# Gated linear attention and a squared-ReLU layer on one core: casting DMA for w_in, transposes moved off TensorE, PSUM banks given out by the scheduler

## The chip, the cores and the metric

The kernel runs on one core of a Trainium2 chip. The metric is the device time of one execution in microseconds (us). Engines are named as in the profile: PE (TensorE matmul), PEld (its weight loads), DVE (VectorE), ACT (ScalarE), POOL (GpSimd), SP (SyncE, which here only issues DMAs).

## The reference

Per batch (4) and head (8), over 768 steps with 48 channels, a state of 48 x 48 decays by alpha and takes up k v; y is q times the state. The heads side by side are x, 3072 tokens of 384, and a layer follows:

```python
for t in range(S):
    state = alpha[:, :, t, :, None] * state + np.einsum('bhd,bhe->bhde', k[:, :, t], v[:, :, t])
    y[:, :, t] = np.einsum('bhd,bhde->bhe', q[:, :, t], state)
...
h = x @ w_in                 # 384 -> 2048
r = np.maximum(h, 0.0)
g = s * (r * r) + b
return (g @ w_out).astype(np.float32)   # 2048 -> 384
```

Inputs and output are float32.

## The kernel before, in words

Tokens go in 24 blocks of 128 (six per batch; block 0, 6, 12 and 18 are the first of a batch). Each block n has one attention part of these steps, four pairs of heads side by side:

- st_ln (ACT, L275): logarithm of alpha. st_cum (PE, L281, L286): its running sum over the block by a triangular matrix, and the sum of all 128 rows, one column for each head pair. st_exp_b and st_exp_i (ACT, L295 to L299): decays, their inverses, and the block's whole decay.
- st_qb, st_kb (DVE, L308, L313): q and k times decay and inverse. st_vcast (POOL, L302): v to bf16, with zeros between the heads of a pair.
- st_T (PE, L324): eight transposes of q and k into PSUM; st_Tcopy (DVE, L344) brings them to SBUF.
- st_KV (PE, L335): k by v, eight matmuls of 64 output rows; st_t1 and st_snew (DVE L354, L356; POOL L364): the new state.
- st_A (PE, L370) and st_mask (DVE, L379): the scores of a block, masked.
- st_y (PE, L414): y already transposed, channels on the partitions, as 12 narrow matmuls in the first block of a batch and 20 in the others, with output tiles of 64 or 32 rows. st_yevac (ACT, L432): y to the bf16 tile xd of its group.

The layer goes by groups of two or four blocks (GROUPS). mm1 (PE, L454) makes a unit of 1536 columns (three k-steps) in one of two PSUM banks h_ps; relu (ACT, L463) and square (DVE, L471, one instruction for each slice of 128 hidden channels) follow. mm2 (PE, L478) sums a block's output in quads of four matmuls; oevac (DVE, L489) scales it by s and adds the bias (b times the column sums of w_out, L262); ostore (SP, L501) stores it. There are 96 units and 96 quads.

Inputs come by SP in 192 KB DMAs (L175), four a block, in packets of 192 bytes, into five buffers each. w_in and w_out come in pieces of 768 KB (L220, L234) through four float32 staging tiles; POOL casts both (L228, L240). In PSUM, cum and the transposes share one bank, KV and y another, st_A has two, h_ps two, o_ps two.

The order on every engine is made at build time by the class Schedule: each step is an op with an engine, a duration, a priority and the resources that it reads and writes. A list scheduler takes the ready op of lowest priority at the earliest time; want(n) gives block n's due time and LEAD how far ahead of its mm1 it is due. Each engine then works its list in order. LOADS is the order of the first loads.

Of the kernel before, what the change touches and what calls it, by code (L numbers as in the profile page):

```python
# [12 lines left out]

VW = 144

GROUPS = [2, 2, 2, 2, 4, 4, 4, 4]
LEAD = {1: 17.0, 2: 20.0, 4: 18.0}

RING = 12

NST = 4

LOADS = ["b0", "b1", "i0", "i1", "b2", "i2", "b3", "i3", "o0", "o1", "o2", "b4", "o3", "b5", "b6"]

class Schedule:
# [12 lines left out]
    def done(self, res, t):  # L40
        self.preset[res] = t

    def op(self, eng, dur, prio, fn, *args, r=(), w=(), lat=0.1):
        me = len(self.ops)
        deps = set()
        start = 0.0
        for x in r:
            if x in self.writer:
                deps.add(self.writer[x])
            start = max(start, self.preset.get(x, 0.0))  # L50
        for x in w:
            if x in self.writer:
                deps.add(self.writer[x])
            deps.update(self.readers.get(x, ()))
        for x in r:
            self.readers.setdefault(x, []).append(me)
        for x in w:
            self.writer[x] = me
            self.readers[x] = []
            self.preset.pop(x, None)  # L60
        self.ops.append((eng, dur, prio, fn, args, deps, lat, start))

    def run(self):
# [10 lines left out]
        for i, o in enumerate(self.ops):  # L74
            free.setdefault(o[0], 0.0)
            ready.setdefault(o[0], [])
            if not left[i]:
                ready[o[0]].append((o[7], i))
        todo = n
        while todo:  # L80
            best = None
            for e, items in ready.items():
                if not items:
                    continue
                t = max(free[e], min(x[0] for x in items))
                _, i = min((self.ops[i][2], i) for a, i in items if a <= t + 1e-9)
# [4 lines left out]
            eng, dur, _, _, _, _, lat, _ = self.ops[i]  # L91
            begin[i] = t
            free[e] = t + dur
            end[i] = t + dur
            todo -= 1
            for u in users[i]:
                left[u] -= 1
                if not left[u]:
                    a = self.ops[u][7]
# [15 lines left out]
def kernel(  # L115
# [23 lines left out]
    NIN = 5  # L139
# [25 lines left out]

# [5 lines left out]
    b_col = sb.tile([128, 1], FP32, name="b_col")  # L171

# [7 lines left out]
    load(0, alpha, a_in)  # L180
    load(0, q, q_in)
    load(0, k, k_in)
    load(0, v, v_in)
    nc.scalar.preload_act_table_set("natural_log_exp_and_others")

    la_sb = many("la", 2, [128, H, 64], BF16, zero=nc.vector)
    U_bf = sb.tile([128, 128], BF16, name="U_bf")
    make_upper_triangular(nc, U_bf, 1.0, diag=True)
    ident_bf = sb.tile([128, 128], BF16, name="ident_bf")
    make_identity(nc, ident_bf)  # L190
    ones_col_bf = sb.tile([128, 1], BF16, name="ones_col_bf")
    nc.vector.memset(ones_col_bf, 1.0)
    vp_sb = many("vp", 3, [128, NP, VW], BF16, zero=nc.gpsimd)
    mask = sb.tile([128, 128], BF16, name="mask")
    make_upper_triangular(nc, mask, 1.0, diag=True)
    b_sb = many("b_s", 2, [128, H, D], FP32)
    binv_sb = many("binv", 2, [128, H, D], FP32)
    qb_sb = many("qb", 2, [128, H, 64], BF16, zero=nc.vector)
    kb_sb = many("kb", 2, [128, H, 64], BF16, zero=nc.vector)
    qkT_sb = many("qkT", 2, [128, 2, NP, 128], BF16)  # L200
    am_sb = many("am", 2, [128, 2, NP, 128], BF16)
    blast_sb = many("blast", 2, [128, NP], BF16)
    t1_sb = many("t1", 2, [128, NP, 96], BF16)
    s_sb = many("s_st", 2, [128, NP, 96], BF16)
    xd_sb = many("xd", 3, [128, 3, 512], BF16)
    r_sb = many("r", 2, [128, 512], BF16)
    gt_sb = [sb.tile([128, RING * C], BF16, name=f"gt{j}") for j in range(NJ)]
    out_sb = many("o_sb", 3, [128, d_model], FP32)

    w_in_bf = sb.tile([128, 3, d_ff], BF16, name="w_in_bf")  # L210
    w_out_bf = sb.tile([128, NJ, d_model], BF16, name="w_out_bf")
    QW = 4 * d_model
    wst = many("wst", NST, [128, QW], FP32)
    colsum = sb.tile([128, 2 * d_model], FP32, name="colsum")
    colpart = sb.tile([128, 2 * d_model], FP32, name="colpart")
    bones = sb.tile([128, 128], FP32, name="bones")
    bias_w = sb.tile([128, d_model], FP32, name="bias_w")

    def load_w_in(i, st):
        nc.sync.dma_start(  # L220
            out=wst[st].rearrange("a (k f) -> a k f", k=3),
            in_=moe_w_in[:, QW // 3 * i : QW // 3 * (i + 1)].rearrange(
                "(k r) f -> r k f", r=128
            ),
        )

    def cast_w_in(i, st):
        nc.gpsimd.tensor_copy(  # L228
            out=w_in_bf[:, :, QW // 3 * i : QW // 3 * (i + 1)],
            in_=wst[st].rearrange("a (k f) -> a k f", k=3),  # L230
        )

    def load_w_out(i, st):
        nc.sync.dma_start(  # L234
            out=wst[st].rearrange("a (j m) -> a j m", j=4),
# [403 lines left out]
```

## Time and profile before

| | us |
|---|---|
| median of 3 runs | 218.08 |
| lowest, highest | 216.7, 219.16 |
| span of the profiled execution | 215.9 |
| PE busy, share of the span | 190.6, 88% |
| DVE busy | 149.3, 69% |
| ACT busy | 100.8, 47% |
| POOL busy | 47.5, 22% |

The span goes from the first to the last instruction of one profiled execution. The page gives no other time of that execution than its span. Busy time of PE is not PE at its peak: matmuls are pipelined, and a matmul at the lower of the two clock levels is busy for longer.

### The profile page before, as it was taken

The page shows a single profiled execution, that of the slowest core. Times are in us where ns is not written, and L with a number is a line of the kernel's source. Part 1 is how long each engine was busy: PE and PEld are TensorE (multiplying, and loading weights), DVE is VectorE, ACT ScalarE, POOL GpSimd, SP SyncE. Part 2 cuts the span into 40 slices and gives each one's busy share as a digit, 9 for nine tenths or more (in the row PEclk, how much of TensorE's full clock was granted, in tenths as well). Part 3 has the DMA queues.
Part 4 walks back from the last instruction along what each step waited for, and adds up shares of the span by engine and source line. Part 5 has one row for each costly group of instructions (what it writes and reads, how often), then busy time and mean ns, then how long its engine had stood idle before and what let it go on. Part 6 is the DMA issues. An engine that isn't in the chain of part 4 may idle for free.

```text
span 215.9 us, 4933 instructions
## 1 busy us (share of the span) xinstructions
PE 190.6 (88%) x1916; PEld 112.4 (52%) x1916; DVE 149.3 (69%) x283; ACT 100.8 (47%) x217; POOL 47.5 (22%) x65
## 2 busy tenths in 40 slices
PE   0167694959999999999999999999999999999993
PEld 0045462535767677756455555545555555555551
DVE  3187269999978787886898868799686963444321
ACT  2313242245655654633787637776365434444200
POOL 8144446635021212111112211002220100000000
PEclk9999998788999999999999999999999999999999
DMA  6999899999499999999977775230110111111122
GB/s 128 189 328 228 189 355 288 241 179 178 98 205 210 211 199 211 196 208 194 218 151 146 148 170 117 44 78 2 36 39 0 39 36 39 37 38 38 39 73 73
DMA packets 107096, 30.21 MB, mean 140 GB/s; under 512 B 100416, under 2 KB 105536, under 8 KB 107072
## 3 DMA queue, kind: packets, MB, share of 16 engines
q1 hardware_dynamic: 107008, 29.89, 59.6%
q8 instruction: 15, 0.25, 0.5%
q14 instruction: 9, 0.07, 0.1%
q0 software_dynamic: 64, 0.00, 0.0%
HBM read 25.17 MB, written 4.72 MB: 138 GB/s over the span
## 4 chain that ended last, share of the span: by engine, by line
PE 51%; DVE 0%; issue 0%
PE o_ps_69 L478 10%; PE h_ps_66 L454 10%; PE o_ps_68 L478 10%; PE h_ps_67 L454 10%; PE py_ps L414 3%; PE ct_ps L324 2%; PE a_ps L370 2%; PE py_ps L335 2%; PE ct_ps L281 1%; PE ct_ps L286 0%; DVE o_sb_169 L489 0%
## 5 line engine op out<-in xcount | busy, mean ns | idle before, releaser
L454 PEld LDWEIGHTS <-w_in_bf 128*128 128x128 bf16 x384 | 36.0, 102 | 23.9 <-issue 3.1
L463 ACT ACTIVATE r_149<-h_ps_66 128x512 bf16<-128x512 f32 x48 | 28.7, 598 | 36.3 <-PE h_ps_66 L454 33.3
L463 ACT ACTIVATE r_150<-h_ps_67 128x512 bf16<-128x512 f32 x48 | 28.8, 599 | 29.1 <-PE h_ps_67 L454 13.2
L454 PE MATMUL h_ps_66<-xd_147,w_in_bf 128*128 128x512 bf16 (+1 forms) x72 | 16.3, 344 | 1.4 <-ACT r_149 L463 1.4
L454 PE MATMUL h_ps_67<-xd_147,w_in_bf 128*128 128x512 bf16 (+1 forms) x72 | 16.7, 352 | 0.0
L379 DVE TENSOR_TENSOR am_139<-a_ps,mask 128x1024 bf16<-128x1024 f32 x12 | 14.7, 1222 | 2.6 <-PE a_ps L370 2.4
L379 DVE TENSOR_TENSOR am_138<-a_ps,mask 128x1024 bf16<-128x1024 f32 x12 | 14.6, 1220 | 1.8 <-PE a_ps L370 1.5
L454 PE MATMUL h_ps_67<-xd_146,w_in_bf 128*128 128x256 bf16 (+1 forms) x72 | 14.4, 333 | 0.7 <-ACT r_150 L463 0.7
L454 PE MATMUL h_ps_66<-xd_146,w_in_bf 128*128 128x256 bf16 (+1 forms) x72 | 15.0, 344 | 0.0
L364 POOL TENSOR_TENSOR s_st_144<-t_142,blast_140 128x384 bf16<-128x384 bf16 x8 | 7.7, 960 | 23.5 <-DVE t_142 L356 16.3
L344 DVE COPY qkT_136<-ct_ps 128x1024 bf16<-128x1024 bf16 x12 | 8.3, 688 | 6.2 <-PE ct_ps L324 5.7
L281 PE MATMUL ct_ps<-la_97,U_bf 128*128 128x384 bf16 x12 | 4.3, 360 | 9.1 <-ACT la_97 L275 9.1
L364 POOL TENSOR_TENSOR s_st_145<-t_143,blast_141 128x384 bf16<-128x384 bf16 x8 | 7.8, 974 | 15.4 <-DVE t_143 L356 13.3
L344 DVE COPY qkT_137<-ct_ps 128x1024 bf16<-128x1024 bf16 x12 | 8.3, 688 | 4.2 <-PE ct_ps L324 4.1
L454 PE MATMUL h_ps_66<-xd_148,w_in_bf 128*128 128x256 bf16 (+1 forms) x48 | 9.8, 327 | 0.0
L454 PE MATMUL h_ps_67<-xd_148,w_in_bf 128*128 128x256 bf16 (+1 forms) x48 | 9.8, 326 | 0.0
L295 ACT ACTIVATE b_s_124<-ct_ps 128x384 f32<-128x384 f32 x12 | 5.9, 491 | 7.9 <-PE ct_ps L286 7.6
L295 ACT ACTIVATE b_s_125<-ct_ps 128x384 f32<-128x384 f32 x12 | 5.9, 490 | 6.1 <-PE ct_ps L286 5.8
L286 PEld LDWEIGHTS <-la_97 128*128 128x128 bf16 x48 | 3.1, 100 | 8.8 <-issue 8.0
L324 PE MATMUL ct_ps<-ident_bf,qb_128 128*128 128x128 bf16 x48 | 5.2, 236 | 2.3 <-DVE qb_128 L308 2.3
L432 ACT ACTIVATE xd_147<-py_ps 128x384 bf16<-128x384 f32 x10 | 4.9, 493 | 4.7 <-PE py_ps L414 4.5
L308 DVE TENSOR_TENSOR qb_128<-q_in_75,b_s_124 128x384 bf16<-128x384 f32 x3 | 1.7, 552 | 7.7 <-ACT b_s_124 L295 7.7
(209 smaller groups left out, 466.9 us busy)
## 6 DMA issues: line engine op xcount, KB each, us to landing
out_dram<-o_sb_167 SPq DMA_DIRECT2D x8, 192.0 KB, 2.3
out_dram<-o_sb_168 SPq DMA_DIRECT2D x8, 192.0 KB, 2.1
out_dram<-o_sb_169 SPq DMA_DIRECT2D x8, 192.0 KB, 1.9
a_in_70<-in_alpha_dram SPq DMA_DIRECT2D x5, 192.0 KB, 4.0
q_in_75<-in_q_dram SPq DMA_DIRECT2D x5, 192.0 KB, 3.8
k_in_80<-in_k_dram SPq DMA_DIRECT2D x5, 192.0 KB, 3.7
v_in_85<-in_v_dram SPq DMA_DIRECT2D x5, 192.0 KB, 4.1
a_in_71<-in_alpha_dram SPq DMA_DIRECT2D x5, 192.0 KB, 3.9
```

Of the source, the lines that this page charges most:

```text
L281: nc.tensor.matmul(out=cum_ps, lhsT=U_bf, rhs=la[:, :, 0:D], start=True, stop=True)
L295: nc.scalar.activation(out=b_sb[n % 2], in_=cum_ps, func=AF.Exp)
L324: nc.tensor.transpose(out=t_ps[:, x, p, :], in_=f[:, 128 * p : 128 * p + 128], identity=ident_bf,)
L335: nc.tensor.matmul(out=p_ps[64 * e : 64 * e + 64, p, :], lhsT=kb[:, 128 * p + 64 * e : 128 * p + 64 * e + 64], rhs=vp[:, p, 48 * e : 48 * ...
L344: nc.vector.tensor_copy(out=qkT_sb[n % 2].rearrange("a x p t -> a (x p t)"), in_=t_ps.rearrange("a x p t -> a (x p t)"),)
L364: nc.gpsimd.tensor_tensor(out=s_sb[n % 2], in0=t1_sb[n % 2], in1=bl, op=ALU.mult)
L379: nc.vector.tensor_tensor(out=am_sb[n % 2].rearrange("a e p t -> a (e p) t"), in0=a_ps.rearrange("a e p t -> a (e p) t"), in1=mask.unsquee ...
L414: nc.tensor.matmul(out=y_ps[32 * (x % 4) : 32 * (x % 4) + 32 * m, x // 4, :], lhsT=(st[:, p, c0 : c0 + 32 * m] if e is None else vp[:, p, ...
L432: nc.scalar.activation(out=xd_sb[g % 3][:, :, t * C : (t + 1) * C], in_=y_ps, func=AF.Copy)
L454: nc.tensor.matmul(out=hp[:, i * n : (i + 1) * n], lhsT=w_in_bf[:, kk, 128 * j : 128 * (j + 1)], rhs=xd_sb[g % 3][:, kk, 0:n], start=(kk = ...
L463: nc.scalar.activation(out=r_sb[w % 2], in_=h_ps[w % 2], func=AF.Relu)
L478: nc.tensor.matmul(out=op[:, 0:d_model], lhsT=gt_sb[j][:, c0 : c0 + C], rhs=w_out_bf[:, j, :], start=(j == 0), stop=(j == NJ - 1),)
```

## The change

- Groups are now 1, 1, 2, 2, 2, 4, 4, 4, 4 blocks, LEAD is one number, and there are nine input buffers of each kind (NIN). The first loads are now ops of the schedule.
- w_in comes by four DMAs on POOL's queue that cast to bf16 on the way (load_w_in); no staging, no cast on POOL. w_out keeps its staging, with its own tile for each piece, and ACT casts it in two halves (cast_w_out).
- st_KV is four matmuls of full width that also make the cross terms between the two heads of a pair; st_sfirst and st_snew, in two halves of 64 partitions, take only the diagonal blocks into the state. It is left out in the last block of a batch. v is cast densely.
- st_y puts tokens on the partitions: four matmuls of 96 columns on the state and eight of 48 columns on the scores. st_yevac copies it to yn. For blocks 0 to 9 PE then transposes y (st_yT, three transposes) and ACT copies it into xd; from block 10 on (N_PE_T) a DMA transpose on SP does it (st_yTdma).
- From block 10 on, q and k are transposed by one DMA on SP (st_Tdma) in place of eight PE transposes and the DVE copy.
- Six PSUM banks are a pool: the scheduler gives one to each use (c, T, P, y, Y, h, o, b) with a limit on how many of each kind may be held. h may hold three.
- square is one instruction for each unit.
- The scheduler models a DMA queue (dma=, BACKLOG).

```diff
-GROUPS = [2, 2, 2, 2, 4, 4, 4, 4]
-LEAD = {1: 17.0, 2: 20.0, 4: 18.0}
+GROUPS = [1, 1, 2, 2, 2, 4, 4, 4, 4]
+LEAD = 24.0
+UNIT = 1.62
 RING = 12
...
-LOADS = ["b0", "b1", "i0", "i1", "b2", "i2", "b3", "i3", "o0", "o1", "o2", "b4", "o3", "b5", "b6"]
+NIN = 9
+N_PE_T = 10
+
+LOADS = ["b0", "i0", "i1", "b1", "i2", "i3", "b2", "o0", "o1", "o2", "o3", "b3"]
...
+    def load_w_in(i):
+        nc.gpsimd.dma_start(
+            out=w_in_bf[:, :, 512 * i : 512 * (i + 1)],
+            in_=moe_w_in[:, 512 * i : 512 * (i + 1)].rearrange("(k r) f -> r k f", r=128),
+        )
...
+    def cast_w_out(i, e):
+        dst = w_out_bf[:, 4 * i + 2 * e : 4 * i + 2 * e + 2]
+        src = wst[i][:, 768 * e : 768 * (e + 1)].rearrange("a (j m) -> a j m", j=2)
+        nc.scalar.activation(out=dst, in_=src, func=AF.Copy)
...
+    def st_Tdma(n):
+        nc.sync.dma_start_transpose(
+            out=qkT_sb[n % 3].rearrange("a x p t -> a (x p) t"),
+            in_=qk_sb[n % 3].rearrange("a x h d -> a (x h d)"),
+        )
...
+        for p in range(NP):
+            nc.tensor.matmul(
+                out=p_ps[:, p, :],
+                lhsT=kb[:, 128 * p : 128 * p + 128],
+                rhs=vb[:, 96 * p : 96 * p + 96],
+                start=True,
+                stop=True,
+            )
...
+        inter = n % NCH != 0
+        if inter:
+            for p in range(NP):
+                nc.tensor.matmul(
+                    out=y_ps[:, 96 * p : 96 * p + 96],
+                    lhsT=qT[:, p, :],
+                    rhs=st[:, p, :],
+                    start=(p == 0),
+                    stop=False,
+                )
+        for h in range(H):
             nc.tensor.matmul(
...
+                out=y_ps[:, 48 * h : 48 * h + 48],
+                lhsT=am[:, h % 2, h // 2, :],
+                rhs=vb[:, 48 * h : 48 * h + 48],
+                start=(h == 0 and not inter),
+                stop=(h == H - 1),
             )
...
+    def st_yTcopy(n):
+        nc.scalar.activation(out=x_of(n), in_=yt_of(n), func=AF.Copy)
+
+    def st_yTdma(n):
+        nc.sync.dma_start_transpose(out=x_of(n), in_=yn_sb[n % 3])
...
+    sched = Schedule(len(banks), {"c": 2, "T": 1, "P": 2, "y": 2, "Y": 1, "h": 3, "o": 2, "b": 1})
...
+            if n < N_PE_T:
+                op("PE", 0.5, t + 0.3, st_T, n, r=[("qb", i3), ("kb", i3)], w=[("T", n)], lat=0.27,
+                   take=("T", n))
+                op("DVE", 0.61, t + 0.4, st_Tcopy, n, r=[("T", n)], w=[("qkT", i3)], drop=("T", n))
+            else:
+                op("SP", 0.5, -3000, st_Tdma, n, r=[("qb", i3), ("kb", i3)], w=[("qkT", i3)],
+                   lat=1.2, dma=1.1)
```

The order that comes of it, at three places. ACT at the start of the program, before; la is the logarithm of a block's alpha, a_in_70 that of block 0, a_in_71 that of block 1:

```order
L184 ACT_TABLE_LOAD
L275 ACTIVATE la_99<-a_in_71 128x8x48
L275 ACTIVATE la_97<-a_in_70 128x8x48
L295 ACTIVATE b_s_124<-ct_ps 128x384
L298 ACTIVATE binv_126<-ct_ps 128x384
```

ACT at the same place now; yn is y of block 0, xd its transposed copy:

```order
L212 ACT_TABLE_LOAD
L302 ACTIVATE la_109<-a_in_70 128x8x48
L323 ACTIVATE b_s_143<-bank_64 128x384
L326 ACTIVATE binv_145<-bank_64 128x384
L327 ACTIVATE blast_152<-bank_64 128x4
L463 ACTIVATE yn_156<-bank_67 128x384
L302 ACTIVATE la_111<-a_in_71 128x8x48
L479 ACTIVATE xd_159<-bank_68 128x3x128
```

The logarithm of block 1 moved from ahead of block 0's to behind block 0's y.

POOL at the start, before, with what each instruction waits for; b_col and s_col are the scalars b and s on all partitions, bones the bias matrix, vp_113 and vp_115 the cast v of blocks 0 and 1:

```order
L528 DMA b_col<-in_moe_b_dram 128x1
L531 DMA s_col<-in_moe_s_dram 128x1
L255 MEMSET bones 128x128
L256 TENSOR_SCALAR bones<-bones,b_col 128x128 [waits DMASW0_49,Pool_49]
L302 CAST vp_115<-v_in_86 128x4x2x48 [waits DMAHW7_49]
L302 CAST vp_113<-v_in_85 128x4x2x48 [waits DMAHW3_49]
L228 CAST w_in_bf<-wst_172 128x3x512 [waits DMAHW0_49]
L228 CAST w_in_bf<-wst_173 128x3x512 [waits DMAHW1_49]
```

And now:

```order
L255 DMA w_in_bf<-in_moe_w_in_dram 128x3x512 x4
L579 DMA b_col<-in_moe_b_dram 128x1
L582 DMA s_col<-in_moe_s_dram 128x1
L283 MEMSET bones 128x128
L284 TENSOR_SCALAR bones<-bones,b_col 128x128 [waits DMASW4_49,Pool_49]
L330 CAST vb_140<-v_in_97 128x384 [waits DMAHW3_49]
L330 CAST vb_141<-v_in_98 128x384 [waits DMAHW7_49]
```

The four loads of w_in stand ahead of the load of b, and the product that waits for b stands, as before, ahead of the first cast of v.

SP in the middle of the program, before; o_sb is a block's output, the a, q, k and v loads are those of later blocks:

```order
L175 DMA v_in_86<-in_v_dram 128x8x48
L501 DMA out_dram<-o_sb_169 128x384
L175 DMA a_in_72<-in_alpha_dram 128x8x48
L175 DMA q_in_77<-in_q_dram 128x8x48
L175 DMA k_in_82<-in_k_dram 128x8x48
```

And now, where the transposes begin; qkT_148 is that of block 10, v_in_101 the v of block 13:

```order
L249 DMA a_in_74<-in_alpha_dram 128x8x48
L249 DMA q_in_83<-in_q_dram 128x8x48
L366 DMA_TRANSPOSE qkT_148<-qk_122 128x8x128
L249 DMA k_in_92<-in_k_dram 128x8x48
L249 DMA v_in_101<-in_v_dram 128x8x48
L366 DMA_TRANSPOSE qkT_149<-qk_124 128x8x128
L249 DMA a_in_75<-in_alpha_dram 128x8x48
L249 DMA q_in_84<-in_q_dram 128x8x48
L249 DMA k_in_93<-in_k_dram 128x8x48
L366 DMA_TRANSPOSE qkT_147<-qk_120 128x8x128
L550 DMA out_dram<-o_sb_165 128x384
```

The transposes stand among the loads on the one list of SP, each behind the loads of a block some three later.

## Rows read from the trace of the kernel before

**Rows 1.** The page: its span, and the bytes moved in 40 equal slices
```profile
span 215.9 us, 4933 instructions
...
GB/s 128 189 328 228 189 355 288 241 179 178 98 205 210 211 199 211 196 208 194 218 151 146 148 170 117 44 78 2 36 39 0 39 36 39 37 38 38 39 73 73
```

**Rows 2.** Busy time by stretch: stretch, length, PE, PEld, DVE, ACT, POOL, clock, DMA
```profile
0.00:24.80 24.80, 9.33 (x111) 6.25 (x111) 11.43 (x20) 6.84 (x16) 12.63 (x24) 1.00 0.91 218
24.80:50.40 25.60, 19.47 (x173) 12.15 (x170) 22.08 (x34) 8.73 (x19) 11.64 (x9) 0.87 0.95 250
50.40:212.50 162.10, 161.81 (x1638) 93.95 (x1635) 115.22 (x230) 85.26 (x182) 23.21 (x32) 1.00 0.51 112
212.50:215.90 3.40, 0.00 (x0) 0.00 (x0) 0.58 (x1) 0.00 (x0) 0.00 (x0) 1.00 0.16 58
```

**Rows 3.** The chain that ended last, in order of time: start, us, what
```profile
106.83 0.46 PE py_ps L414 x12
107.29 0.75 PE h_ps_66 L454 x3
108.04 0.45 PE ct_ps L324 x8
108.49 0.65 PE h_ps_67 L454 x3
109.14 0.29 PE py_ps L335 x8
109.43 0.75 PE h_ps_66 L454 x3
110.18 0.33 PE a_ps L370 x8
110.51 0.27 PE ct_ps L281
110.78 0.08 PE ct_ps L286 x4
110.86 0.67 PE h_ps_67 L454 x3
...
112.83 0.62 PE py_ps L414 x20
```

**Rows 4.** Groups by line: the bias matmuls (busy us, mean ns, idle before)
```profile
L262 PE MATMUL o_ps_69<-colsum,bones 128*128 128x384 f32 x4 | 1.5, 486 | 0.0
```

**Rows 5.** The instructions of the first 25 us, in order of time
```profile
0.73 0.43 SPq L175 DMA_DIRECT2D a_in_70<-in_alpha_dram  x1
...
8.13 0.52 ACT L275 ACTIVATE la_99<-a_in_71 128x384 bf16<-128x384 f32 x1 [6.13 <-DMA a_in_71<-in_alpha_dram]
...
14.78 0.76 PE L414 MATMUL py_ps<-am_138,vp_113 128*64 128x128 bf16 x12 [0.87 <-DVE am_138 L379]
...
24.85 1.46 PE L454 MATMUL h_ps_66<-xd_146,w_in_bf 128*128 128x256 bf16 x6
```

**Rows 6.** DMA issues of the first 30 us: size, us from issue to landing
```profile
a_in_70<-in_alpha_dram SPq DMA_DIRECT2D x1, 192.0 KB, 2.8
...
b_col<-in_moe_b_dram POOLq DMA_DIRECT2D x1, 0.5 KB, 3.2
```

**Rows 7.** Busy time in the stretch of the block loads
```profile
60.00:110.00 50.00, 49.78 (x592) 32.23 (x590) 40.13 (x85) 27.38 (x61) 8.77 (x13) 1.00 0.98 204
```

**Rows 8.** The instructions of DVE and POOL from 32 us, in order of time
```profile
32.26 2.26 POOL L240 CAST w_out_bf<-wst_172 128x1536 bf16<-128x1536 f32 x1 [0.60 <-DMA wst_172<-in_moe_w_out_dram]
...
33.11 1.55 DVE L471 TENSOR_TENSOR gt_153<-r_150 128x256 bf16<-128x256 bf16 x1
```

**Rows 9.** The page's groups by line: relu
```profile
L463 ACT ACTIVATE r_149<-h_ps_66 128x512 bf16<-128x512 f32 x48 | 28.7, 598 | 36.3 <-PE h_ps_66 L454 33.3
```

**Rows 10.** The page's groups by line: the copy of the transposed q and k
```profile
L344 DVE COPY qkT_136<-ct_ps 128x1024 bf16<-128x1024 bf16 x12 | 8.3, 688 | 6.2 <-PE ct_ps L324 5.7
```

**Rows 11.** The page: the DMA queue of SP (packets, MB, share of 16 engines)
```profile
q1 hardware_dynamic: 107008, 29.89, 59.6%
```

More of the change, by code (lines that the diff above doesn't have):

```diff
@@ L74, in run, with start @@
         for i, o in enumerate(self.ops):
-            free.setdefault(o[0], 0.0)
+            free.setdefault(o[0], 0.7)
             ready.setdefault(o[0], [])
             if not left[i]:
-                ready[o[0]].append((o[7], i))
-        todo = n
+                ready[o[0]].append((0.0, i))
+        idle = {b: 0.0 for b in range(self.banks)}
+        held = {k: 0 for k in self.most}
+        drops = dict(self.drops)
+        until = {}
+        queue = 0.0
+        todo = n
+        def start(a, i):
+            take = self.ops[i][8]
+            if take is None:
+                return a
+            if not idle or held[take[0]] >= self.most[take[0]]:
+                return None
+            return max(a, min(idle.values()))
         while todo:
@@ L203 @@
[L203 to L213, printed above, removed]
@@ new lines, in st_sfirst @@
+    def st_sfirst(n):
+        p_ps = p_of(n)
+        for e in range(2):
+            rows, cols = half(e)
+            nc.vector.tensor_tensor(
+                out=s_sb[n % 2][rows, :, cols],
+                in0=p_ps[rows, :, cols],
+                in1=blast_sb[n % 2][rows].unsqueeze(2).to_broadcast([64, NP, D]),
+                op=ALU.mult,
+            )
+    def st_t1(n):
+        nc.vector.tensor_tensor(
+            out=t1_sb[n % 2], in0=p_of(n), in1=s_sb[(n - 1) % 2], op=ALU.add
+        )
@@ L441 @@
         for u in range(NJ // per):
-            units.append((g, [u * per + i for i in range(per)]))
+            units.append((g, u * per, per))
         for tt in range(m):
@@ new lines @@
+            if not last:
+                op("PE", 0.2, t + 0.35, st_KV, n, r=[("kb", i3), ("vb", i3)], w=[("P", n)], lat=0.27,
+                   take=("P", n))
+            if first:
+                op("DVE", 0.6, t + 0.5, st_sfirst, n, r=[("P", n), ("bl", i2)], w=[("S", i2)],
+                   drop=("P", n))
+            elif not last:
+                op("DVE", 0.48, t + 0.5, st_t1, n, r=[("P", n), ("S", 1 - i2)], w=[("t1", i2)],
+                   drop=("P", n))
+                op("POOL", 1.1, t + 0.1, st_snew, n, r=[("t1", i2), ("bl", i2)], w=[("S", i2)])
@@ L586 @@
             unit_i += 1
[L587 removed]
+            j0 = units[w][1]
+            js = range(j0, j0 + per)
             t = w * UNIT
[L589 to L593 removed]
+            op("PE", 0.66, t, mm1, w,
+               r=[("xd", g % 3, x) for x in range(m)] + [("wib", j0 // 4)],
+               w=[("h", w)], lat=0.27, take=("h", w))
+            op("ACT", 0.5, t + 0.5, relu, w, r=[("h", w)], w=[("r", w % 2)], drop=("h", w))
+            op("DVE", 0.36, t + 1.0, square, w, r=[("r", w % 2)],
                w=[("gt", x, j) for j in js for x in ring])
```

435 lines of the change are left out of this document (209 added, 226 removed), and 5 rows, old and new, of the table Y_PARTS.

## The prediction

> **What bounds the kernel now.** I read the page's slices first, then the stretches, the chain that ended last, the waits of PE, and last the DMA views. [...] From 50.4 us on PE is busy 161.81 of 162.10 us at a granted clock of 1.00, while DVE has 115.22 and ACT 85.26 of it [rows 2]: here only PE's own work counts. [...] After 212.5 us there are 3.4 us of last eviction and store. The DMA engines move 128 to 355 GB/s in the first ten slices, so they hardly pause [rows 1, 2].
>
> The chain tells what a piece of PE work costs when nothing waits: its pieces stand end to end. A unit of mm1 is 0.65 us after full-width work, but 0.75 after st_KV or st_y, whose tiles are 64 or 32 columns wide: a change of tile form costs 0.10. So a block's attention costs: transposes 0.45, st_KV 0.29 + 0.10, st_A 0.33, cum 0.27 + 0.08 (the 0.27 holds the 0.10 behind st_A), st_y 0.62 + 0.10, or 0.46 + 0.10 in the first block of a batch [rows 3]. With 0.02 of rounding that is 2.26, or 2.10 in the four first blocks. PE's whole work before: 24 x 2.26 - 4 x 0.16 = 53.6, 192 units and quads x 0.65 = 124.8, the bias matmuls 1.5 [rows 4]: 179.9 us.
>
> **PE work, removed and added.** The four matmuls of one column behind cum take 0.08 + 0.02, that is 25 ns for a pair of weight load and matmul of full width; a transpose of 128 columns takes 0.45 / 8 = 56 ns [rows 3]. By columns a matmul of 96 costs 42 ns, one of 48 costs 21, for which I take the 25. st_KV has now 4 x 42 = 0.17 and no change of form: -0.22. st_y has 4 x 42 + 8 x 25 = 0.37 for 20 narrow ones: -0.35. Blocks 0 to 9 gain three transposes of y, 3 x 56 = +0.17: together -0.40 a block. Blocks 10 to 23 lose the eight transposes, -0.45: together -1.02. Four last blocks lose st_KV altogether, another 0.17 each. Sum: 10 x 0.40 + 14 x 1.02 + 4 x 0.17 = 19.0 us; 160.9 remain. The bounds of it: if each narrow pair costs the 56 ns of a transpose, st_KV saves 0.17 and st_y 0.05, and the sum is 10.8. Below, with 21 ns, it is 19.8. I take 25 because it is a measured row of the same kind of weights.
>
> [...]
>
> **The start.** Before, the first logarithm on ACT is that of block 1 and waits 6.13 us for its alpha; block 0's y starts at 14.78 and the first mm1, which needs block 1 as well, at 24.85 [rows 5]. Now block 0's logarithm stands first, its alpha lands at 0.73 + 2.8 = 3.5 us [rows 5, 6], and a group of one block needs no second. But this is not what sets the steady part; data are. A load of 192 KB at the 204 GB/s of the stretch full of loads [rows 7] takes 0.96, a block 3.84; a 768 KB piece of weights at the 355 GB/s of the best slice [rows 1] takes 2.2. Bytes begin at about 2.5 (3.5 less one load). Order: b0, w_in, b1, b2, w_out, b3. Block 3 is in at 2.5 + 4 x 3.84 + 8 x 2.2 = 35.5. On PE's list cum of block 6 stands ahead of the first mm1 of blocks 2 and 3, so alpha of block 6 is wanted: 35.5 + 2 x 3.84 + 0.96 = 44.1, then 0.52 of logarithm [rows 5] and 0.7 of cum and st_A ahead of mm1: PE runs on from 45.5.
>
> By then it has done mm1 and mm2 of blocks 0 and 1 (16 x 0.65 = 10.4), the bias 1.5, blocks 0 to 3 (4 x 1.86, less 0.17 in the first) 7.3, parts of 4 to 6 some 2.3: 21.5 us. Left: 139.4.
>
> The casting DMA's price is not in the trace. From below it is the 2.2 of a plain piece; from above, 768 KB at the loads' 204 GB/s, 3.9. I take 2.2, the row of the same piece; the upper end puts the start off by 6.8. POOL: four descriptor jobs stand ahead of b_col, s_col, the bias product and vcast of block 0. The product waits for b_col, 3.2 us to landing before [rows 6] and now behind 3 MB in its queue, so to about 15; behind it wait vcast, KV and y of block 0, and with them, in order, PE. mm1 of block 0 then starts at about 19 and not 12. The cover is the wait for block 6 at 45.5: some 17 us of work are left for 26 us, so I cost it at nothing, at most 3.
>
> POOL's w_out cast stood beside a square of 1.55 us on DVE [rows 8]; both go. The casts on ACT are 8 x 768 columns; at relu's 598 ns for 512 [rows 9] 0.9 each, 7.2 us, hidden in the stretch where ACT is busy 8.73 of 25.6 [rows 2]. One square of 512 columns for two of 256 and no Tcopy in 14 blocks lighten DVE: 115.2 - 14 x 0.69 (its row, [rows 10]) = 105.5 over 139.4, 76%. It still fits, but nearer to PE: I add 2 us of gaps (0 to 4) and 2.5 us of low clock behind the start (19.47 x 0.13, [rows 2]; the same sort of start).
>
> **The DMA transposes.** 256 KB for q and k and 96 KB for y, 14 times, on SP's queue. The trace has none. From below: 352 KB at 355 GB/s, 1.0 us. From above: in pieces of 32 bytes, 11,264 packets at 0.596 x 16 x 215.9 / 107,008 = 19.2 ns each on 16 engines [rows 11], 13.5 us. Between ends so far apart I go by the row of the block loads, 352 KB at 204 GB/s = 1.7, and take 1.6. A block then costs the queues 3.84 + 0.55 (store) + 1.6 = 6.0, PE 5.2 + 1.24 = 6.4: it just fits. Blocks 0 to 9 are in at 2.5 + 17.6 + 38.4 + 1 = 59.5, block 23 at 59.5 + 13 x 6.0 = 138. Its chain (exponentials, transposes, mask, y) is about 13: 151. PE comes to the last group's mm1 45 pieces x 0.65 = 29 us before its end, at about 160. So 9 us of slack. SP takes its list in order: a transpose waits for kb or y of its block, and the loads and stores behind it wait too; nine input buffers instead of five cover that.
>
> [...]
>
> **The sum.** 45.5 + 139.4 + 2.5 + 2 + 3.4 = 192.8 us of span. The page gives only the span of its execution, 215.9; the median of the runs, 218.08, lies 2.2 above it. So 195.
>
> **Rivals.**
> 1. Narrow matmuls cost a full pitch of 56 ns. For it: nothing else in the trace has 48 columns under 128-wide weights. Against: the 25 ns. 10.8 saved and not 19.0: 203.
> 2. The queues set the pace. With T for both transposes of a block the end moves by 13 x (T - 1.6) - 9 once this is positive. T = 3.0 gives 204. For it: 6.0 against 6.4 is no margin, and before the queues are full from 60 to 110 us [rows 7]. Against: the slack.
> 3. Slower: the transposes go in small pieces. Place: SP's queue, blocks 10 to 23; price by the same formula; it passes 218 at T = 4.1 and is 1% slower at 4.2. T = 8 gives 269, 13.5 gives 341. [...] Against: no row; but even the loads, the smallest packets here, move 204 GB/s. [...]
> 4. Better: no gaps, no low clock, the start 2 us earlier: 188.
> That the change doesn't do what it says can only be for its start: the logarithm of block 1 might still hold it, but ACT's list has block 0's first.
>
> **Chances.** Forecast 0.52, rival 1 0.12, rival 2 0.17, rival 3 0.09, rival 4 0.10. The runs before lie 1.1% apart, so 1% is about what a measurement can tell from no change. Faster takes all but rival 3 and the far end of rival 2 (0.03, T about 4): 0.88, within 1% 0.03, slower 0.09. The range reaches from just under rival 4, 187, to rival 2 at T = 3.8, 214; outside stay rival 3, and a few in a hundred at either end.
>
> **What would show it.** PE idle of under 4 us from about 46 us to the end; st_y at about 0.4 and st_KV at 0.2 in the chain; b_col landing near 15 us and vcast of block 0 behind it; transposes landing in 2 to 6 us; PE's waits in the second half for ACT's relu at most. It is wrong if mm1 of a late group waits for a DMA, if the stretch from 140 to 165 us shows idle PE, or if PE starts its steady part past 52 us.

## The result and the profile after

The changed kernel takes 206.67 us (median of 4 runs, 206.11 to 207.96) beside 217.39 (216.22 to 219.16) for the kernel before in the same comparison: a ratio of 0.950 with a 95% interval of 0.944 to 0.956. It is faster, by 10.7 us; the forecast of 195 stood for some 22. Batches of runs are compared below by their ratio to the kernel before; times are medians of all runs, and a ratio leaves out runs over 1.5% above the fastest of their kernel, unless said otherwise.

The page of the changed kernel, its span, PE's line, and the slices of the DMA engines with what they moved; [rows 1] has the same of before:

```profile
span 204.4 us, 4279 instructions
...
PE 167.6 (82%) x1594; PEld 107.4 (53%) x1594; DVE 131.7 (64%) x240; ACT 107.8 (53%) x235; POOL 39.7 (19%) x76
...
DMA  6999999999999999999999799999964221111122
GB/s 131 175 189 195 270 379 209 188 209 227 189 211 188 216 205 191 188 211 178 159 224 184 148 204 206 176 204 209 201 138 109 61 59 40 40 42 38 38 77 77
...
q1 hardware_dynamic: 126016, 31.80, 75.3%
q0 software_dynamic: 1664, 1.57, 4.8%
```

PE's busy time fell from 190.6 to 167.6 us, but its share of the span too, from 88 to 82%: PE has become idle somewhere. The DMA engines stay nearly full until about 148 us (29 of 40 slices). Where PE is idle shows in the stretches, to be held beside [rows 2]; the columns are busy us of each engine with its instructions, granted clock, DMA share and GB/s:

```profile
core 0: us, PE busy (x) PEld busy (x) DVE busy (x) ACT busy (x) POOL busy (x), PEclk, DMA share, GB/s
...
8.40:19.10 10.70, 0.06 (x2) 0.09 (x1) 1.23 (x1) 0.00 (x0) 1.07 (x2) 1.00 1.16 195
19.10:49.65 30.55, 23.89 (x305) 18.88 (x306) 24.59 (x41) 21.08 (x45) 7.46 (x11) 1.00 1.01 246
49.65:81.00 31.35, 31.34 (x407) 25.39 (x408) 30.86 (x55) 24.85 (x62) 9.63 (x17) 1.00 1.00 199
81.00:156.00 75.00, 65.17 (x592) 37.02 (x590) 52.86 (x98) 42.96 (x98) 14.69 (x27) 1.00 0.99 185
156.00:200.97 44.97, 44.93 (x277) 24.59 (x275) 17.85 (x39) 16.16 (x28) 0.00 (x0) 1.00 0.18 56
```

PE works without a pause from 49.65 to 81 us and from 156 us to its end at 200.97. Between them, where the kernel before had 49.78 us of 50 busy as late as 60 to 110 [rows 7], it loses 9.8 of 75.00 us, and the DMA share is 0.99. PE's waits say for what (us in total, times, longest):

```profile
PE bank L376 <- POOL vb L330: 10.7, 1, 10.7
PE a_ps L417 <- DMA qkT<-qk: 9.1, 9, 1.6
```

The second is st_A waiting for a DMA transpose, nine times. The first, the stall in the start, is taken up below. PE's timeline around one of these waits (start, us, line, operation, instructions, idle before and its releaser):

```profile
97.72 0.33 PE L376 MATMUL bank<-vb,qk 128*128 128x96 bf16 x4
97.89 0.81 PE L502 MATMUL bank<-xd,w_in_bf 128*128 128x512 bf16 x3
98.53 0.33 PE L442 MATMUL bank<-s_st,qkT 128*128 128x96 bf16 x4
98.70 0.36 PE L450 MATMUL bank<-vb,am 128*128 128x48 bf16 x8
98.91 0.81 PE L530 MATMUL bank<-w_out_bf,gt 128*128 128x384 bf16 x4
99.56 0.81 PE L502 MATMUL bank<-xd,w_in_bf 128*128 128x512 bf16 x3
101.88 0.40 PE L417 MATMUL a_ps<-qkT 64*128 64x128 bf16 x8 [1.51 <-DMA qkT<-qk]
102.21 0.82 PE L530 MATMUL bank<-w_out_bf,gt 128*128 128x384 bf16 x4
102.87 0.81 PE L502 MATMUL bank<-xd,w_in_bf 128*128 128x512 bf16 x3
```

The differences of the starts are the prices: st_KV 0.17, st_y 0.17 + 0.21 = 0.38, a unit of mm1 0.64; [rows 3] has what they cost before. And at 101.88 the reader sees the loss: st_A of block 14 waits 1.51 us, and behind it stand a quad and a unit that need nothing of this block, but PE's list is in order. Where its transpose was until then is told by DVE's last instruction ahead of it (k times the inverse decay) and by SP's issue of it:

```profile
91.19 0.55 DVE L341 TENSOR_TENSOR qk<-k_in,binv 128x384 bf16<-128x384 f32 x1
97.78 2.05 SPq L366 DMA_TRANSPOSE qkT<-qk  x1
```

Its data are ready at 91.74, SP comes to it 6 us later, at 97.78, and it lands at 101.83. The transposes of q and k of 13 of the 14 blocks stand ready 2 to 8 us before SP issues them; from issue to landing they take 3.1 to 5.6 us.

The chain that ended last goes through the start and through these transposes (start, us, what):

```profile
3.95 2.33 POOL w_in_bf L255 x3
6.29 11.52 DMA b_col<-in_moe_b_dram
17.99 0.61 POOL bones L284
18.60 0.48 POOL vb L330
19.12 0.48 PE bank L376 x4
...
97.78 4.05 DMA qkT<-qk
...
102.10 4.00 DMA qkT<-qk
```

### The profile page after: what moved, and what is told of

Its sections match the earlier page's. It is cut to its first block, busy times and chain, and to the rows that moved or that the text cites. A ratio compares the mean times of both kernels' runs of the same rounds, so it can differ in the third digit from the quotient of the medians.

```text
span 204.4 us, 4279 instructions
## 1 busy us (share of the span) xinstructions
PE 167.6 (82%) x1594; PEld 107.4 (53%) x1594; DVE 131.7 (64%) x240; ACT 107.8 (53%) x235; POOL 39.7 (19%) x76
## 3 DMA queue, kind: packets, MB, share of 16 engines
q1 hardware_dynamic: 126016, 31.80, 75.3%
## 4 chain that ended last, share of the span: by engine, by line
PE 56%; DMA 26%; DVE 7%; issue 4%; POOL 3%; ACT 3%; SPq 0%; POOLq 0%; ACTq 0%; DVEq 0%
PE bank L530 23%; PE bank L502 22%; DMA qkT<-qk 19%; DMA b_col<-in_moe_b_dram 6%; PE a_ps L417 3%; PE bank L353 2%; POOL w_in_bf L255 2%; DMA a_in<-in_alpha_dram 1%; PE bank L450 1%; DVE colpart L272 1%; DVE am L426 1%; PE bank L309 1%; PE bank L376 1%; ACT r L511 1%; DVE gt L523 1%
## 5 line engine op out<-in xcount | busy, mean ns | idle before, releaser
L502 PE MATMUL bank<-xd,w_in_bf 128*128 128x512 bf16 (+2 forms) x432 | 76.5, 315 | 0.7 <-DMA xd<-yn 0.5
L511 ACT ACTIVATE r<-bank 128x512 bf16<-128x512 f32 x96 | 56.6, 604 | 35.7 <-PE bank L502 26.7
L530 PE MATMUL bank<-w_out_bf,gt 128*128 128x384 bf16 x384 | 73.7, 326 | 0.0
L523 DVE TENSOR_TENSOR gt<-r 128x512 bf16<-128x512 bf16 x96 | 41.9, 448 | 23.7 <-ACT r L511 23.3
L530 PEld LDWEIGHTS <-gt 128*128 128x128 bf16 x384 | 35.7, 98 | 25.3 <-issue 0.2
L426 DVE TENSOR_TENSOR am<-a_ps,mask 128x1024 bf16<-128x1024 f32 x24 | 29.3, 1219 | 11.7 <-PE a_ps L417 11.5
L406 POOL TENSOR_TENSOR s_st<-t,blast 64x192 bf16<-64x192 bf16 x32 | 19.3, 603 | 43.7 <-PE bank L442 11.7
L539 DVE SCALAR_TENSOR_TENSOR o_sb<-bank,s_col,bias_w 128x384 f32<-128x384 f32 x24 | 14.7, 613 | 13.9 <-PE bank L530 13.9
L463 ACT ACTIVATE yn<-bank 128x384 bf16<-128x384 f32 x24 | 11.9, 496 | 17.8 <-PE bank L450 17.7
L333 DVE TENSOR_TENSOR qk<-q_in,b_s 128x384 bf16<-128x384 f32 x24 | 13.9, 579 | 4.3 <-ACT b_s L323 4.3
L376 PE MATMUL bank<-vb,qk 128*128 128x96 bf16 x80 | 6.8, 209 | 10.7 <-POOL vb L330 10.7
L341 DVE TENSOR_TENSOR qk<-k_in,binv 128x384 bf16<-128x384 f32 x24 | 14.4, 598 | 0.4 <-DMA k_in<-in_k_dram 0.4
L376 PEld LDWEIGHTS <-qk 128*128 128x128 bf16 x80 | 4.9, 99 | 12.8 <-issue 10.8
```

Of the source, the lines that this page charges most:

```text
L333: nc.vector.tensor_tensor(out=qk_sb[n % 3][:, 0, :, 0:D], in0=q_in[n % NIN], in1=b_sb[n % 2], op=ALU.mult,)
L341: nc.vector.tensor_tensor(out=qk_sb[n % 3][:, 1, :, 0:D], in0=k_in[n % NIN], in1=binv_sb[n % 2], op=ALU.mult,)
L376: nc.tensor.matmul(out=p_ps[:, p, :], lhsT=kb[:, 128 * p : 128 * p + 128], rhs=vb[:, 96 * p : 96 * p + 96], start=True, stop=True,)
L406: nc.gpsimd.tensor_tensor(out=s_sb[n % 2][rows, :, cols], in0=t1_sb[n % 2][rows, :, cols], in1=blast_sb[n % 2][rows].unsqueeze(2).to_broad ...
L426: nc.vector.tensor_tensor(out=am_sb[n % 2].rearrange("a e p t -> a (e p) t"), in0=a_ps.rearrange("a e p t -> a (e p) t"), in1=mask.unsquee ...
L502: nc.tensor.matmul(out=hp[:, i * n : (i + 1) * n], lhsT=w_in_bf[:, kk, 128 * j : 128 * (j + 1)], rhs=xd_sb[g % 3][:, kk, 0:n], start=(kk = ...
```

## Experiments

Two theories stood after the result. Q: the DMA queues, full until 150 us, set the pace, and 14 transposes lengthen them. Rivals: the late start (b_col landing at 17.8 us) is carried to the end; or a transpose is late by its own latency. The first four runs part them.

**b_col first.** The DMAs of b_col and s_col are issued ahead of w_in on POOL:

```diff
-            op("POOL", 0.7, t + 30, lambda: nc.gpsimd.dma_start(out=b_col, ...), w=["b"], lat=2.0)
+            op("POOL", 0.7, t + 30, lambda: None, w=["b"], lat=2.0)
...
+    nc.gpsimd.dma_start(out=b_col, in_=moe_b.to_broadcast((128, 1)))
+    nc.gpsimd.dma_start(out=s_col, in_=moe_s.to_broadcast((128, 1)))
     sched.emit()
```

> b_col and s_col are issued ahead of the four pieces of w_in on POOL; nothing else moves. Both theories: b_col lands before 7 us, block 0's vcast, KV and mm1 start about 9 us earlier, PE's stall of 10 us at KV of block 0 goes. Theory Q (queues): the DMA queues are full from 5 to 156 us whatever PE does, the last blocks' qkT lands when the queues have worked off their bytes, so the end stays: 206.7 +- 1 (ratio to the kernel before 0.946 to 0.956), and PE's idle between 81 and 156 us grows by about what the start gains (10 to 13 or 14 us). Rival S (the late start is simply carried to the end, and the idle at A is the in-order issue of the transposes): 4 us less, 202.5 (0.932).

Measured: 206.81 us, ratio 0.942 (0.936 to 0.949). The stall went, the end hardly moved:

```profile
8.40:19.10 10.70, 6.87 (x64) 5.25 (x60) 2.40 (x4) 2.93 (x7) 0.31 (x1) 1.00 1.22 200
...
81.00:156.00 75.00, 65.27 (x592) 36.96 (x590) 52.42 (x97) 42.65 (x98) 14.55 (x27) 1.00 0.92 186
```

PE has 6.87 us of work in the stretch where it had 0.06, and as before some 9.7 us of idle between 81 and 156 us; the idle did not grow as theory Q had it. The ratio is just below the 0.946 to 0.956 that theory Q had; its interval overlaps that range and the changed kernel's, and the 4 us of the rival are outside it.

**All transposes on PE**, alone and with b_col first:

```diff
-N_PE_T = 10
+N_PE_T = 24
```

> All 24 blocks transpose on PE, as blocks 0 to 9 do; no DMA transpose is left. PE's work grows by 14 x (0.45 + 0.17) = 8.7 us. Theory Q: 14 x 2.4 = 34 us of queue time go, PE has under 2 us of idle from 50 us on, the 10 us of waits for qkT are traded for 8.7 of work: 206 (204 to 208), a tie; the DMA share of 110 to 156 us falls from 0.97 to under 0.6. Rival N (the waits for the transposes don't matter, the narrow matmuls or bank waits cost): PE's idle stays and the time grows by the whole 8.7, to 215.

> Both edits: b_col first, and no DMA transpose. Theory Q: with the queues out of the way the earlier start is worth its full 4 us, so 202 (200 to 204), less than either edit alone, PE idle after 50 us under 2 us. Rival S: 4 us below whatever the run with PE transposes alone gives, and the first edit alone gives the 4 too. If the start gives nothing here either, the steady part is set by the arrival of block 6's data and not by block 0.

Measured: 204.69 us, ratio 0.934 (0.930 to 0.938), and 204.71, ratio 0.935 (0.932 to 0.938). As the changed kernel stands, its DMA transposes cost it some 3 us over doing the same on PE. Of the run with PE transposes alone:

```profile
81.00:156.00 75.00, 75.00 (x759) 47.02 (x757) 63.31 (x115) 50.36 (x114) 15.02 (x27) 1.00 0.59 128
...
q1 hardware_dynamic: 105408, 26.75, 58.8%
```

No idle is left, against rival N. The queue's row gives the price of the transposes in this kernel: 0.753 x 204.4 - 0.588 x 203.4 = 34.3 us over 14 blocks, 2.45 us a block for 352 KB. That the earlier start is worth nothing even with free queues was not the forecast; more on it below.

**Light loads.** The loads of blocks 10 to 23 are cut to one head:

```diff
+        hs = H if n < 10 else 1
         nc.sync.dma_start(
-            out=dst[n % NIN],
-            in_=src[b, :, c * C : (c + 1) * C, :].rearrange("h s d -> s h d"),
+            out=dst[n % NIN][:, 0:hs],
+            in_=src[b, 0:hs, c * C : (c + 1) * C, :].rearrange("h s d -> s h d"),
```

> Loads of blocks 10 to 23 carry one head of eight (the other seven heads of the tile keep an earlier block's numbers, so the work on them is the same but on other data); all 28 DMA transposes stay, in the same places of SP's list. Queue time falls by 14 x 4 x 7/8 x 0.96 = 47 us. Theory Q: the waits of st_A for qkT all but vanish (under 2 us), PE is busy through the stretch and the span falls by 8 to 10 us: 197 (195 to 199), ratio 0.905. Rival L (each transpose is late by its own latency and by SP issuing in order, not by the bytes in front of it): the waits stay at 6 us or more and the time above 203.

Measured: 194.84 us, ratio 0.891 (0.888 to 0.895).

```profile
81.00:156.00 75.00, 75.00 (x678) 43.33 (x676) 58.14 (x108) 48.64 (x108) 15.38 (x27) 1.00 0.49 100
...
qkT<-qk SPq DMA_TRANSPOSE x14, 3.1
xd<-yn SPq DMA_TRANSPOSE x14, 2.3
```

All 28 transposes are there, landing in 3.1 and 2.3 us, and PE waits for none. Their own latency is out as the cause: what is ahead of them delays them. Whether that is bytes or issues this run does not part, for the light loads also hold SP for less (59.6 us of issues in the stretch, for 69.3).

**The planner's price.** Still, the queue had room at the end: it empties at about 150 us and PE works to 201. In the class Schedule the two transposes cost 1.1 + 0.5 = 1.6 us of queue, and PE's list is fixed by that at build time.

```diff
-                   lat=1.2, dma=1.1)
+                   lat=1.2, dma=1.75)
...
-                op("SP", 0.5, -3000, st_yTdma, n, r=[("yn", i3)], w=[xd], lat=1.2, dma=0.5)
+                op("SP", 0.5, -3000, st_yTdma, n, r=[("yn", i3)], w=[xd], lat=1.2, dma=0.7)
```

> The planner's price of the two DMA transposes is set to what the traces gave (1.75 for q and k and 0.70 for y, 2.45 us a block, for 1.1 and 0.5), and nothing else: the same 14 blocks go by DMA, and PE's and SP's lists are written in another order. Theory O (no slack is left because PE's list is fixed for transposes of 1.6 us: each later block is 0.8 us late, 13 x 0.85 = 11 us, and mm1 that stands behind st_A can't step in): with the list written for 2.45 the waits at st_A fall under 3 us and the time to 199 to 202. Rival Q0 (the queues' bytes alone set the end, whatever the order): 206.7 +- 1.5.

Measured: 198.27 us, ratio 0.907 (0.901 to 0.913). Two numbers in the planner are worth 4.3% of the time before, with the same instructions, the same bytes and the same queues in another order:

```profile
81.00:156.00 75.00, 72.60 (x635) 41.23 (x632) 56.12 (x101) 44.74 (x101) 14.97 (x26) 1.00 0.97 190
...
PE a_ps L417 <- DMA qkT<-qk: 1.6, 2, 1.0
```

Both lists moved. On SP's, the transposes of q and k of blocks 11 to 22 stand behind one to five loads fewer. On PE's, more units and quads stand ahead of st_A of the late blocks, of 192 in all (counted in the lists; the third line is a run further down):

```
block                  10  12  14  16  18  20  22  23
changed kernel (1.6)   44  52  68  85  93 111 123 129
true price (2.45)      45  54  71  88 102 120 137 143
price 3.0              46  54  72  94 108 127 140 149
```

The last st_A, of block 23, starts at nearly the same time in the changed kernel and with the true price:

```profile
159.16 0.40 PE L417 MATMUL a_ps<-qkT 64*128 64x128 bf16 x8
159.52 0.40 PE L417 MATMUL a_ps<-qkT 64*128 64x128 bf16 x8
```

So the last transpose comes no sooner; what differs is that PE has by then done 14 pieces more, 14 x 0.65 = 9.1 us of work, and the span is 8.7 us shorter (204.4 to 195.7). How much PE's list would give alone, with SP's as it was, was not run.

**Fewer transposes by DMA**, N_PE_T = 16, with the old prices and with the true ones:

> Blocks 10 to 15 transpose on PE too (6 x 0.62 = 3.7 us of PE work more), 16 to 23 by DMA. The loads are through at about 122 us with no transposes, so 8 x 2.45 = 20 us more ends at 142, ahead of PE. Theory O and Q alike: waits for qkT under 3 us, 204.7 (all on PE) - 8 x 0.62 = 200 (199 to 202). If a late transpose costs PE as much as in the changed kernel (0.7 us a block): 205.

> Both: 16 blocks on PE and the true price in the planner. Theory O: no waits for qkT to speak of, 199.5 (198 to 201), at most 1 us below the run with 16 on PE alone. Rival Q0: the same as that run.

Measured: 203.73 us, ratio 0.929 (0.923 to 0.935), and 201.37, ratio 0.921 (0.915 to 0.928). Both are above their ranges: 3.1 us of waits stay in the first, and even 1.9 in the second. Their intervals overlap, and the price hardly moves the list here: 132 and 133 pieces stand ahead of the last st_A. With true prices 14 blocks by DMA (0.907) beat 8 (0.921), so once the list fits, moving six more blocks off PE pays.

**More transposes**, into spare tiles:

```diff
+        nc.sync.dma_start_transpose(out=spare_q, in_=qk_sb[n % 3][:, 0].rearrange("a h d -> a (h d)"))
...
         nc.sync.dma_start_transpose(out=x_of(n), in_=yn_sb[n % 3])
+        nc.sync.dma_start_transpose(out=spare_y, in_=yn_sb[n % 3])
```

> Behind each DMA transpose of q and k, q's half is transposed once more into a spare tile, and behind each of y, y once more: 224 of 352 KB a second time, which nobody reads; the planner knows nothing of it. Queue time by 2.45 us a block: 224/352 x 2.45 = 1.56 us more. Theory Q and O: no slack is left, so the end moves by 13 x 1.56 = 20 us: 227 (222 to 232), a slower kernel than before. If the transposes were late by latency and not by queue time, the end moves by SP's issue alone: under 215.

Measured: 234.51 us, ratio 1.070 (1.065 to 1.076): the sign is right, but the end moves by (1.070 - 0.950) x 217.4 = 26 us and not by 20, and the engines are not full:

```profile
81.00:156.00 75.00, 59.18 (x473) 31.92 (x472) 39.38 (x74) 32.80 (x75) 9.52 (x18) 0.86 0.85 167
...
q1 hardware_dynamic: 139456, 35.01, 71.3%
```

q1's time grew by only 0.713 x 232.1 - 153.9 = 11.6 us, 0.83 us a block and not 1.56: the price by the queue's time is not a constant. Something else may pace, and SP is near full: its issues that touch this stretch add up to 71.2 us beside its 75, 1.2 to 1.6 us for each transpose. In the changed kernel they add up to 69.3 (12 transposes of q and k 21.2, 12 of y 18.5, 38 loads 23.9, 10 stores 5.8). PE ran its pieces there at a granted clock of 0.86, which may be part of the 26 us. So a new rival: SP's issuing and not the engines' time is what a transpose costs. Four runs ask that:

```diff
+        eng = nc.gpsimd if n >= 10 and (dst is k_in or dst is v_in) else nc.sync
-        nc.sync.dma_start(
+        eng.dma_start(
```

> The changed kernel with k's and v's loads of blocks 10 to 23 issued by POOL in place of SP; the same bytes, the planner's prices as in the changed kernel. SP is relieved of 28 issues of about 0.65 us, 20 of them (13 us) between 81 and 156 us, where it is occupied for 69 of 75 us. Theory B (the DMA engines' time is what a transpose takes; they are 0.99 busy there): waits at st_A stay at 8 us or more, 206.7 +- 2. Rival I (SP's issuing is what paces: a transpose holds SP for 1.2 to 1.8 us): the waits fall under 4 us and the time to 199 to 202.

> The same move of k's and v's loads, with the planner's true price of 2.45 us a block. Theory B: 198.3 +- 1.5, as without the move. Rival I: no waits for transposes are left at all, 2 us less at most, 196 to 197, since PE's idle after 50 us is only 2.4 us with the true price.

Measured: with the old prices 204.14 us, ratio 0.933 (0.922 to 0.943); with the true ones 198.07, ratio 0.904 (0.900 to 0.909). The four runs of the first lie far apart, 200.92, 202.62, 205.66 and 208.60 us, and its ratio is of all four; the lower two are 0.92 of the kernel before. The profile is of the lowest:

```profile
81.00:156.00 75.00, 72.01 (x666) 41.85 (x664) 58.14 (x107) 47.15 (x105) 30.67 (x45) 1.00 1.04 192
...
PE a_ps L418 <- DMA qkT<-qk: 1.6, 3, 0.7
```

With the bytes and PE's list unchanged the waits for qkT fall from 9.1 to 1.6 us. The lower two runs are what rival I had (waits under 4 us, 199 to 202), and theory B's 8 us of waits are not there; the upper two runs have no profile, so what held them is open. The last qkT lands at 152.2 us in place of 157.7. With the true price nothing is gained that can be told, as theory B had it, but only 1.6 us of waits were left there to gain. Then issues with next to no bytes, and bytes without issues on SP:

```diff
+        if n >= 10:
+            x = (q_in, k_in, v_in, a_in).index(dst)
+            nc.sync.dma_start(out=tiny[x], in_=q[0, 0, x : x + 1, :])
```

> The changed kernel with a DMA of 192 bytes on SP's queue behind each load of blocks 10 to 23, into tiles that nobody reads: four more issues a block of about 0.45 us, 1.8 us of SP and next to no bytes. Rival I (SP's issuing paces): SP has 5.7 of 75 us to spare, that is 0.4 us a block, so 13 x 1.4 = 18 us more: 225. Theory B (the engines' time paces): 207 to 210.

```diff
+        if n >= 10 and dst is v_in:
+            nc.gpsimd.dma_start(out=spare, in_=src[b, :, c * C : (c + 1) * C, :].rearrange("h s d -> s h d"))
```

> The changed kernel with v of blocks 10 to 23 loaded once more, on POOL's queue, into a tile that nobody reads: 192 KB a block, 0.96 us of the engines, no issue on SP. Theory B: 13 x 0.96 = 12 us more: 219. Rival I: 206.7 to 209.

Measured: 214.37 us, ratio 0.981 (0.977 to 0.985), and 219.72, ratio 1.003 (0.998 to 1.008). Against 0.950 that is 6.7 and 11.4 us. The stretch from 81 us of the one, then of the other:

```profile
81.00:156.00 75.00, 62.17 (x543) 34.77 (x542) 47.29 (x88) 39.01 (x90) 12.74 (x24) 0.95 0.91 172
```

```profile
81.00:156.00 75.00, 60.67 (x533) 34.27 (x530) 45.11 (x84) 37.48 (x86) 20.17 (x31) 0.95 1.07 195
```

The bytes cost what theory B had (11.4 of 12), the issues 6.7 where rival I had 18 and theory B at most 3. So neither theory holds alone: more bytes and more issues both move the end, and fewer issues on SP, with the same bytes, take the waits away. How much of a late transpose is the engines' time and how much SP's list is not shown; the loads given to POOL left SP's issuing and their place ahead of the transposes in its queue at once.

**Once more the start, with the true price**: b_col first (the edit above), and the small first groups undone (GROUPS = [2, 2, 2, 2, 4, 4, 4, 4]).

> True price, and b_col and s_col ahead of w_in. PE's stall of 10 us at KV of block 0 goes. If block 6's data (alpha lands at about 45.6) and the chain behind it set the steady part: 198.3 +- 1, and PE's early work is spread over the idle it had. Rival: the stall is carried to the end now that the transposes no longer hide it: 194.5 (4 us less).

> True price, and the groups as before, 2, 2, 2, 2, 4, 4, 4, 4: the small first groups alone undone. If the start is set by block 6's data, the first mm1 comes later (when block 1 is in, about 25 us), and the work of two blocks moves behind it: at most 3 us more, 198 to 201. Rival: the small groups carry the start, 4 us or more: 202 to 206.

Measured: 198.57 us, ratio 0.909 (0.903 to 0.915), and 198.93, ratio 0.909 (0.904 to 0.913). Neither differs from 0.907 by more than the noise: b_col's stall costs nothing, and the small first groups bring nothing, that can be told.

**A price that is too high**, dma=2.15 and 0.85:

> The planner's price of the two transposes at 3.0 us a block (2.15 and 0.85), above the 2.45 of the traces. Theory O: too high a price only moves st_A further behind, PE has other work there: within 1.5 us of the run at 2.45, 197.5 to 200. Rival: the lists must fit the true price, and a list for 3.0 runs out of mm1 or holds the loads back: 201 or more.

Measured: 199.19 us; the four runs are 196.22, 197.12, 201.27 and 201.33, and the ratio 0.900 (0.896 to 0.904) is of the lower two. By these it is level with the true price or a little better, by the median level; the upper two are at the rival's 201, and what sets them apart is not shown. A price of 1.6 was too low; 3.0 does no harm that can be told, and it is ahead of both kernels.

## Why the prediction was wrong

The sign was right and the size was not: 206.67 is 11.7 us above 195. The forecast had PE's end at 45.5 + 139.4 + 2.5 + 2 = 189.4; measured is 49.65 (start of the steady part) + 141.4 (busy time of the three stretches from there) + 9.9 (idle in them) = 200.97. So 4.2 from the start, 2.0 from the work, 9.9 - 4.5 from idle against the allowances, and 0.1 behind PE's end and to the median, which were right (204.4 + 2.3). Of the prediction's own signs of being wrong one came: PE idle between 140 and 165 us (2.7 us, two waits for qkT).

- **The step that failed is "so 9 us of slack".** It was worked out from the end: block 23's chain done at 151, PE at the last group's mm1 at about 160. That holds if PE may do other work while a transpose is late. It may not: its list is written at build time for transposes of 1.6 us, and st_A of every block but one stands just where its qkT is due by that price. At 2.45 us each block is by estimate 0.85 later than the one before, 13 x 0.85 = 11 us, and PE was idle for 9.8. The slack was in the queues, and PE's list had none. The run with the true price shows it: with lists that can use the slack, PE's idle from 49.65 us on falls to 2.4, where rival 2's formula leaves 13 x 0.85 - 9 = 2. That the same formula's 197 also comes near the measured 198.3 is in part luck: it lacks the start's 4.2 and the work's 2.0, and it holds 4.5 of allowances that did not come.
- **T = 1.6 us** was mis-sized: 2.45 us of queue time, 352 KB at 147 GB/s, where I had gone by the loads' 204 [rows 7]; and that row gives 1.77, so 1.6 was below it without a reason. With 2.45 a block costs the queues 3.84 + 0.55 + 2.45 = 6.8 and not 6.0, beside PE's 6.4: "it just fits" goes too. The 2.45 lay within the bounds of 1.0 and 13.5; the pieces of 32 bytes behind the 13.5 were my assumption, and no run shows them: the transposes of the 14 blocks added 126016 - 105408 = 20608 packets and 31.80 - 26.75 = 5.05 MB to the queue, 245 bytes a packet. I had named T = 3 and more as a rival and a price of 1.6 as covered; the planner's own 1.6 beside my 1.6 should have told that the list has no margin for any other T. The transposes were slower than the loads in packets of 192 bytes, 147 GB/s beside 204. Rival 3, which passes 218 only at T = 4.1, was out by the 2.45.
- **SP's list** was put at nothing ("nine input buffers instead of five cover that"). The transposes stood 2 to 8 us on it with their data ready, and giving 28 of its loads to POOL took 7.5 of the 9.1 us of waits away in the profiled run. So part of what I price as 2.45 us of queue time may be SP's time; the runs do not part the two.
- **PE work.** st_KV 0.17 and st_y 0.38 were forecast as 0.17 and 0.37: the narrow pairs run at 0.21 / 8 = 26 ns, and rival 1 is out. Eight transposes of 128 columns took 0.46 (52.74 to 53.20), 57 ns each, for the 56 of the forecast. Not counted was a change of tile form from st_y to st_A, which stands right behind it in some places, 0.29 in place of 0.21 (52.12 to 52.41 in the timeline). The work left came to 141.4 for 139.4.
- **The start.** The chain was as told: b_col landed 11.5 us after its issue behind w_in, at 17.8 and not 15, vcast, KV and mm1 behind it (mm1 at 21.6 for 19). "I cost it at nothing" was right, as the three runs with b_col first show. The steady part began at 49.65 and not 45.5. Alpha of block 6 was issued at 41.83 and in at 45.83, 1.7 behind the forecast 44.1. But its logarithm started only at 48.23, with no wait for the load: ACT's list has it behind the exponentials and the y of earlier blocks, and that y came late because PE had waited 1.01 us for its mask. From the end of the logarithm to 49.65 are 0.9 us, as forecast. So the data set the start only in part; with b_col first and PE transposes, where alpha of block 6 was issued at 42.85, mm1 ran on from 48.37. That this 4 us could be had back by another order of the first loads was not tried.
- **Allowances.** The low clock (2.5) did not come in the steady part: the granted clock is 1.00 in each stretch from 8.4 us on. In the kernel before it reads 0.50 from 37 to 40 us and 1.00 from 41 to 44; six matmuls of 256 columns took 1.44 us at 38.78 and 0.82 at 41.53. (Before the steady part of the changed kernel, 36 matmuls of 128 columns took 3.96 us from 21.58 on, and the next 12 took 0.83; what was slow there lay ahead of a wait of 1.78 us.) Gaps (2) came nearly all as the waits for transposes; ACT's casts and the denser DVE cost nothing that shows.

What the casting DMA by itself is worth was not tried; its four pieces took 0.048 x 204.4 = 9.8 us of the engines, 2.45 each, near the 2.2 taken.

## What to carry to other kernels

Where an engine's order is written at build time by a cost model, slack of a resource is worth nothing to an engine whose list was written for a lower price: read the model's price of each new operation, and ask what happens if the chip's is higher by half. Price a DMA by the queue's time with and without it, look at how long it holds the engine that issues it as well, and give the planner that price or a higher one; 1.6 for 2.45 lost 4 to 5% here, 3.0 lost nothing that could be told. And a stall ahead of a stretch that waits for data anyway can be free, however long it looks on the chain: b_col's 11.5 us stood on the chain that ended last, and taking it away gave nothing that could be told, in three pairs of runs.

## What was not expected of the hardware

- A DMA of 0.5 KB on POOL's queue landed 11.5 us after its issue when four casting pieces of w_in stood ahead of it, and 3.4 us after it when it went first (the run with the true price and b_col first).
- A transpose holds SP for longer than a load: 1.76 us for q and k and 1.54 for y on the mean between 81 and 156 us, beside 0.63 for a load (23.9 / 38). With 224 KB of transposes more a block the engines' time grew by 11.6 us and the time by 26.
- PE was slower where it had started earlier. In the run with PE transposes and b_col first 12 matmuls of 128 columns took 1.44 us at 22 us; with b_col late the same 12, at 25.7 us, took 0.83:

```profile
22.15 1.44 PE L502 MATMUL bank<-xd,w_in_bf 128*128 128x128 bf16 x12
```

```profile
25.71 0.83 PE L502 MATMUL bank<-xd,w_in_bf 128*128 128x128 bf16 x12
```

The granted clock of both stretches (19.1 to 49.65 us) reads 1.00, so the profile doesn't say why; in the first PE had worked in pieces with idle between them since 8 us, in the second it had stood still for 10.8 us and then worked with short pauses. The run with b_col first alone shows the same 1.44, at 22.47 us, and its granted clock reads 0.94 in that stretch. By the first mm1 of 256 columns, the steady part, the early start of 9.7 us was down to 1.1 us (48.37 for 49.42), and by 81 us to next to nothing (733 matmuls begun and 730): while the loads keep the DMA engines full (DMA share 1.00 and 0.99 in that stretch), PE only reaches the next wait sooner.
